# Pooled values of attention split into 112 and 32 tokens, a third column product in an accumulator's bank, and a new issue order

## The chip, the core and the metric

One kernel on one core of a Trainium2 chip. The metric is the device time of one execution in microseconds (us), from the first to the last instruction with the start and end around them. The core has five engines that run their own instruction streams in order: TensorE (PE, matmuls; its weight loads are listed apart as PEld), VectorE (DVE), ScalarE (ACT), GpSimd (POOL) and SyncE (SP, which here only issues transfers). They wait for one another by semaphores.

## The reference

Three layers on 4 x 576 tokens of 512 channels. Attention first, of 32 heads (16 pairs of heads, here called pairs 0 to 15):

```python
q_d = q.reshape(B, H, Sd, factor, D).mean(axis=3)      # factor 4, Sd = 144
k_d, v_d = ...                                          # the same for k and v
out_up = np.repeat(sm_attn(q_d, k_d, v_d), factor, axis=2)
mask = np.abs(pos[:, None] - pos[None, :]) < factor
out_local = softmax(where(mask, scale * q @ k.T, -1e9)) @ v
x = out_up + out_local
```

then a gated layer, `h = relu(x @ w_in)`, `gate = sigmoid(conv3(h))`, `x = (h * gate) @ w_out`, and a mixer, `u = x + (x.T @ U @ V).T`, `out = u + relu(u @ w_ch1) @ w_ch2`. Everything is float32.

## The kernel before

All engines' instructions are written out by hand: `SEQ` is a string of words, and each word calls one small function, so the order of the words is the order of the instructions on each engine. A word is a name with numbers, `V.3.2` is `pv_local(3, 2)`. The words that matter here, p being a pair of heads:

- `lq.p`, `lr.p`, `lw.p` load q and k (576 KB), the values for pooling (`vr`, 288 KB) and the values for the local part (`vw`, 384 KB). `wl.1.i` loads a weight tile (512 KB). All loads go through `load` (L319) on SP's queue, in the order of the words; each waits until those more than 900 units before it have landed, and also for the engine that last read the buffer it overwrites.
- `S.p` scores of the local part (L447 masks, L454 48 small matmuls, each two records in the trace), `dp.p` (L483) and `D.p` (L476) subtract the maxima, `E.p` exponentials, `R.p re.p r.p` row sums, their eps and their reciprocals, `n.p` or `nv.p` the normalisation, `T.p` (L554) three transposes, `c.p` or `cv.p` the copy out of PSUM, `V.p` (L588) 24 matmuls with `vw`.
- `Sd.p` (L520), `Md.p`, `Ed.p` (L532), `nd.p` on POOL or `ndv.p` on DVE (L537) the same for the pooled part with its 144 tokens. `Td.p` (L561) transposes the 96 x 144 weights in six pieces of 72 columns, `cd.p` on ACT or `cdv.p` on DVE (L578) copies them out, `vs.p.i` on POOL or `vsv.p.i` on DVE (L544, L547) sums the four tokens of `vr` in two steps on 72 partitions (tokens 0 to 71 and 72 to 143 beside each other), and `Vd.p` (L596) is four matmuls on 72 partitions. `x.p` (L615) adds both parts into X.
- `1.n.c` (`g1`, L813) is a quarter, three matmuls, of the n-th column product of the gated layer, into one of two PSUM banks, `gx` for even n and `gy` for odd (`gtile`). Its chain on ACT and DVE is `r1.n` (L819), `c0.n` (L835), `c1.n.k` (L840), `th.n` (L844), `gt.n` or `gm.n` (L851), `gh.n` (L856) and `gl.n` on POOL or `gL.n` on DVE (L859). The first eight products use `gt`, which leaves the result in the same PSUM bank until `gL.n` has read it, so product n + 2 can begin only after `gL.n`; `gm` moves it to SBUF. `2.n.c` (`g2`, L867) multiplies the gated block with w_out into accumulators `acc0` to `acc2`, one PSUM bank each.
- `f.n` issues n beats (L389, `beat`), matmuls without a use that are put where PE would stand still; there are 89 in the list. `sp` (L371) is the same ahead of the first loads.

From product `1.0.0` on, attention of the later pairs is interleaved with the column products. After attention and the gated layer come the mixer's stages (L1024, L1056, L1177), whose weights pass through DRAM.

Of the kernel before, what the change touches and what calls it, by code (L numbers as in the profile page):

```python
# [7 lines left out]
F32 = mybir.dt.float32  # L8
# [10 lines left out]
SEQ = ("lq.1 xz sf sp.1 k sp.0 K qs.1 sp.1 S.1.1 lc cw.0 z M.1 lq.0 qs.0 qd.1 Sd.1.0 dp.1 lr.0 E.1 R.1 S.0.2 M.0 vs.0.0 "  # L19
# [253 lines left out]


@with_exitstack
def mixer_kernel(ctx, tc, consts, qk, vw_, vr_, w1, w2, cw_, u_, v_, out, outT):
    nc = tc.nc
    DM = out.shape[1]
    S = qk.shape[3]
# [526 lines left out]
    def g1(n, cc):  # L806
        g, f = divmod(n, NF)
        wd = runs(g)[1]
        if cc == 0:
            gp[n] = gtile(n % 2)  # L810
# [481 lines left out]
```

## Time and profile before

| | |
|---|---|
| time, median of 3 runs | 708.25 us (705.76 to 709.41) |
| the profiled execution's own time | 708.66 us |
| its span, first to last instruction | 706.9 us |
| PE busy | 686.0 us (97%) |
| PE weight loads busy | 630.0 us (89%) |
| DVE busy | 542.2 us (77%) |
| ACT busy | 430.6 us (61%) |
| POOL busy | 348.2 us (49%) |
| mean granted clock of TensorE | 0.992 of 2.4 GHz |
| transfers | 152 MB, 215 GB/s on average |

PE is busy for all but 20.9 us of the span. Times below are us from the span's start. Busy time of an engine is the union of its records; an idle time in a timeline is what lay ahead of the group, with what released it. "issue" means that the engine waited for nothing that the profile shows.

### The profile page before, as it was taken

Reading aid. Unit: us, or ns where it says so; the run is one execution under the profiler, and the core shown is the slowest. Engines: PE = TensorE matmul, PEld = TensorE weight load, DVE = VectorE, ACT = ScalarE, POOL = GpSimd, SP = SyncE. Lnnn points to the kernel's source line nnn. Section 1 sums busy time; section 2 is a strip of 40 time slices with the busy share of each in tenths; the row PEclk is TensorE's granted clock in tenths of the full one; section 3 lists DMA queues with packets and bytes.
Section 4 is the critical chain, followed back from the end, with each engine's and each line's share of the span. In section 5 each row is a group of like instructions: output and inputs, shape, how many; then the busy total and the mean of one; then the engine's idle time right before and its main releaser. Section 6 shows DMA issues by size and latency. Waiting matters only on the chain.

```text
span 706.9 us, 15817 instructions
## 1 busy us (share of the span) xinstructions
PE 686.0 (97%) x5937; PEld 630.0 (89%) x5937; DVE 542.2 (77%) x961; ACT 430.6 (61%) x995; POOL 348.2 (49%) x353
## 2 busy tenths in 40 slices
PE   7868999999999999999999999999999999999997
PEld 5767889888888889898899898899999999999997
DVE  5867999989887776989976856667767798666777
ACT  3777897866696676888655655654343565344431
POOL 2335557542353643467555645253733564544544
PEclk9979999999999999999999999999999999999999
DMA  7877723763553221145778898998687666787865
GB/s 203 275 245 250 266 77 104 242 206 126 169 185 132 74 75 62 60 163 194 254 270 308 285 329 280 298 318 317 230 263 230 249 226 238 231 279 223 283 200 185
DMA packets 74620, 152.09 MB, mean 215 GB/s; under 512 B 8112, under 2 KB 16560, under 8 KB 74544
## 3 DMA queue, kind: packets, MB, share of 16 engines
q1 hardware_dynamic: 74544, 151.09, 64.5%
q8 instruction: 47, 0.77, 0.4%
q14 instruction: 29, 0.24, 0.1%
HBM read 111.21 MB, written 39.85 MB: 214 GB/s over the span
## 4 chain that ended last, share of the span: by engine, by line
PE 81%; DMA 7%; DVE 5%; issue 2%; ACT 2%; POOL 2%; SPq 0%; DVEq 0%; POOLq 0%; ACTq 0%
PE g L1024 22%; PE acc L867 13%; PE g L813 12%; PE xa L1177 9%; PE acc L1056 9%; PE ya L1177 5%; PE za L1177 2%; PE O L588 1%; DMA zraw<-in_w_dram 1%; PE h L891 1%; DMA vr<-in_vr_dram 1%; PE O L596 1%; PE S L454 1%; PE Sd L520 1%; DMA raw<-in_w_dram 1%
## 5 line engine op out<-in xcount | busy, mean ns | idle before, releaser
L1024 PE MATMUL g<-bt,as 128*128 128x384 f32 x1008 | 195.7, 338 | 0.0
L1024 PEld LDWEIGHTS g<-bt,as 128*128 128x128 f32 x1008 | 178.4, 188 | 4.1 <-ACT tp L1029 0.3
L813 PE MATMUL g<-xhl,w 128*128 128x386 f32 (+1 forms) x576 | 116.9, 346 | 1.6 <-DVE ghl L859 1.6
L867 PE MATMUL acc<-w,ghl 128*128 128x512 f32 x432 | 114.2, 397 | 0.0
L813 PEld LDWEIGHTS g<-xhl,w 128*128 128x128 f32 x576 | 102.6, 191 | 7.0 <-DVE ghl L859 1.8
L1163 POOL TENSOR_TENSOR rt<-fr,rt 128x384 fp32r<-128x384 f32 x64 | 66.5, 1050 | 72.8 <-ACT rt L1159 49.5
L1184 DVE TENSOR_TENSOR uT<-uT,xa 128x384 f32<-128x384 f32 x128 | 68.6, 550 | 29.4 <-PE xa L1177 29.1
L867 PEld LDWEIGHTS acc<-w,ghl 128*128 128x128 f32 x432 | 79.3, 188 | 13.0 <-issue 0.4
L1177 PE MATMUL xa<-rt,wb 128*128 128x384 f32 x384 | 82.4, 338 | 2.0 <-DVE uT L1184 1.2
L859 POOL TENSOR_TENSOR ghl<-ct,ghl 128x384 fp32r<-128x384 f32 x40 | 42.9, 1073 | 78.8 <-ACT ghl L856 74.7
L1029 ACT ACTIVATE tp<-g 128x384 f32<-128x384 f32 x72 | 35.1, 488 | 73.4 <-PE g L1024 71.3
L1056 PE MATMUL acc<-w,a 128*128 128x512 f32 x288 | 73.8, 394 | 0.5 <-DVE a L1044 0.5
L1033 DVE TENSOR_TENSOR tp<-g,tp 128x384 f32<-128x384 f32 x72 | 40.0, 555 | 43.2 <-PE g L1024 35.0
L840 DVE SCALAR_TENSOR_TENSOR g<-h,cw,g 128x384 f32<-128x384 f32 x96 | 59.4, 619 | 17.5 <-ACT g L835 16.0
L1163 POOL TENSOR_TENSOR rt<-tp,rt 128x384 fp32r<-128x384 f32 x48 | 50.4, 1057 | 45.0 <-ACT rt L1159 23.1
L1177 PEld LDWEIGHTS xa<-rt,wb 128*128 128x128 f32 x384 | 67.8, 188 | 3.5 <-DVE uT L1184 2.6
L1056 PEld LDWEIGHTS acc<-w,a 128*128 128x128 f32 x288 | 53.2, 188 | 9.6 <-DVE a L1044 0.9
L1159 ACT ACTIVATE rt<-fr 128x384 fp32r<-128x384 f32 x64 | 31.8, 520 | 22.8 <-PE za L1177 8.0
L1177 PE MATMUL ya<-rt,wb 128*128 128x384 f32 x192 | 42.6, 339 | 0.4 <-DVE uT L1184 0.3
L1086 POOL TENSOR_TENSOR l<-s,l 128x256 fp32r<-128x256 f32 x28 | 23.6, 845 | 34.1 <-ACT l L1082 29.8
L1184 DVE TENSOR_TENSOR uT<-uT,ya 128x384 f32<-128x384 f32 x64 | 34.8, 549 | 5.7 <-PE ya L1177 5.5
L819 ACT ACTIVATE h<-g 128x386 f32<-128x386 f32 (+1 forms) x48 | 23.5, 489 | 23.2 <-PE g L813 23.0
(169 smaller groups left out, 1266.4 us busy)
## 6 DMA issues: line engine op xcount, KB each, us to landing
as<-s SPq DMA_DIRECT2D x112, 256.0 KB, 3.3
wb<-t SPq DMA_DIRECT2D x112, 256.0 KB, 4.4
s<-as SPq DMA_DIRECT2D x56, 256.0 KB, 3.0
raw<-in_w_dram SPq DMA_DIRECT2D x26, 512.0 KB, 7.6
zraw<-in_w_dram SPq DMA_DIRECT2D x22, 512.0 KB, 3.5
qk<-in_qk_dram SPq DMA_DIRECT2D x16, 576.0 KB, 6.0
t<-l SPq DMA_DIRECT2D x28, 256.0 KB, 2.7
vw<-in_vw_dram SPq DMA_DIRECT2D x16, 384.0 KB, 3.7
```

Source lines behind the costliest of these rows:

```text
L813: nc.tensor.matmul(gp[n][:, :wd], w[:, a, cc], xhl[g, cc][:, b, :wd], start=cc == 0 and i == 0, stop=cc == NCC - 1 and i == 2)
L840: nc.vector.scalar_tensor_tensor(out=o, in0=inner(g, hts[n], k), scalar=cw[:, k * NF + f:k * NF + f + 1], in1=o, op0=ALU.mult, op1=ALU.add)
L859: eng.tensor_tensor(ghl[n][:, 1], cts.pop(n), ghl[n][:, 0].bitcast(F32), op=ALU.subtract)
L867: nc.tensor.matmul(acc[g][c], t[:, a, c * P:(c + 1) * P], w[:, b], start=f == 0 and i == 0, stop=f == NF - 1 and i == 2)
L1024: nc.tensor.matmul(o, w[:, a, k], Bs[r, j, k][:, b, :TB], start=j in (0, 1, 3) and n == 0, stop=n == 3 * HC - 1, skip_group_check=True)
L1029: nc.scalar.activation(out=t[:, :TB], in_=bank[q, 0][:, :TB], func=AF.Copy)
L1033: nc.vector.tensor_tensor(t, bank[q, 1][:, :TB], t, op=ALU.add)
L1056: nc.tensor.matmul(acc2[g][c], t[:, a, c * P:(c + 1) * P], w[:, b], start=f == 0 and n < 2 and i == 0, stop=f == NFP - 1 and n >= 2 and i ...
L1159: nc.scalar.activation(out=t[:, 0], in_=f_src(q, j), func=AF.Copy)
L1163: eng.tensor_tensor(t[:, 1], f_src(q, j), t[:, 0].bitcast(F32), op=ALU.subtract)
L1177: nc.tensor.matmul(o, w[:, a, m * P:m * P + P], t[:, b], start=new and i == 0, stop=i == 2, skip_group_check=True)
L1184: nc.vector.tensor_tensor(u, u, src, op=ALU.add)
```

## The change

**Pooled values.** Tokens 0 to 111 of a pair now stand on 112 partitions, and the other 32 tokens of four pairs together on 128 partitions (pair p on partitions 32 (p mod 4) onwards). The host writes two inputs: `vr`, 112 partitions x 2 KB a pair (224 KB), and `vz` for pairs 0, 4, 8 and 12, 128 partitions x 4 KB (512 KB), which holds that pair's 112 tokens and the 32 tokens of its four pairs. `vsum` therefore works on half the columns for twelve pairs, and for the four others on 128 partitions. `Td.p` transposes columns 0 to 127 in one piece, and in the other the columns from 112 - 32 (p mod 4) to 143, 32 to 128 of them, so that the last 32 land on the right partitions. `copy_Td` is two copies, 112 x 288 and 32 x 288, but one of 128 x 576 where p mod 4 is 3. `Vd.p` stays four matmuls of 64 x 144, over 112 and 32 partitions.

**Third product.** Product 2 is written to a bank with the tag `acc2`, not `gx`; it uses `gm.2`, which moves its result to SBUF, since `2.0.2` takes this bank.

**Order.** All of `SEQ` is new. It has the same words as before, but for `gm.2` in place of `gt.2`, and the same 89 beats.

```diff
     def load_vr(p):
-        t = st[p]["vr"] = xu.tile([72, 4, 2, 2, D], F32, name="vr", tag=f"xu{4 + p % 2}")
-        load(t.rearrange("p t h c d -> p (t h c d)"), vr_[p], 288)
+        if p % 4:
+            t = st[p]["vr"] = xu.tile([NM, 4, 2 * D], F32, name="vr", tag=f"xu{4 + p % 2}")
+            load(t.rearrange("p t x -> p (t x)"), vr_[p], 2 * NM)
+        else:
+            t = st[p]["vr"] = xu.tile([P, 4, 4 * D], F32, name="vr", tag=f"xu{4 + p % 2}")
+            load(t.rearrange("p t x -> p (t x)"), vz_[p // 4], 512)
...
     def vsum(p, part, eng=None):
...
-            d = e["vd"] = pa.tile([72, 2, 2, D], F32, name="vd", tag="vd", bufs=2)
-            eng.tensor_tensor(d.rearrange("p h c d -> p (h c d)"), t[:, 0], t[:, 1], op=ALU.add)
+            d = pa.tile([P, 4 * D], F32, name="ve", tag="ve", bufs=1)
+            e["vd"] = d[:NM]
+            for i in range(p, p + 4):
+                st[i]["ve"] = d[:, 2 * D:]
+        eng.tensor_tensor(d, t[:, 0], t[:, 1], op=ALU.add)
...
+    def rest(p):
+        return slice(32 * (p % 4), 32 * (p % 4) + 32)
...
     def trans_d(p, n):
-            for c in range(2):
-                nc.tensor.transpose(s[:72, c, 96 * j:96 * j + 96], e["Pd"][:, j, 72 * c:72 * c + 72], ident[:96, :96])
+            nc.tensor.transpose(s[:, 0, to], e["Pd"][:, j, :P], ident[:96, :96])
+            nc.tensor.transpose(s[:rest(p).stop, 1, to], e["Pd"][:, j, NM - rest(p).start:], ident[:96, :96])
...
     def copy_Td(p, copy):
-        copy(t, e.pop("Td")[:72, :, :288])
+        if rest(p).stop == P:
+            copy(t, s[:, :, :288])
+        else:
+            copy(t[:NM, 0], s[:NM, 0, :288])
+            copy(t[rest(p), 1], s[rest(p), 1, :288])
...
     def pv_pooled(p):
-            for c in range(2):
-                nc.tensor.matmul(e["O"][...], e["vd"][:, h, c], pt[:, c, :, 48 * h:48 * h + 48], start=c == 0, stop=c == 1)
+            nc.tensor.matmul(o, e["vd"][:, cols], pt[:NM, 0, :, to], start=True, stop=False)
+            nc.tensor.matmul(o, e["ve"][rest(p), cols], pt[rest(p), 1, :, to], start=False, stop=True)
...
     def g1(n, cc):
-            gp[n] = gtile(n % 2)
+            gp[n] = gtile(n % 2) if n != 2 else pools["psg"].tile([P, 512], F32, name="g", tag="acc2")
```

On PE, after the scores of pairs 1 and 0 (`Sd.0` and `dp.0` are the first two rows). Before:

```order
L520 MATMUL Sd<-ss,qd_100 96x144 x3
L483 MATMUL S<-nm,front 128x192 x2
L389 MATMUL S<-mask,identR 128x224 x15
L447 MATMUL S<-mask,identR 128x192 x2
L454 MATMUL S<-qk 24x32 x48
L554 MATMUL T<-front,P 128x128 x3
```

Now:

```order
L525 MATMUL Sd<-ss,qd_100 96x144 x3
L488 MATMUL S<-nm,front 128x192 x2
L575 MATMUL Td<-front,Pd 128x96
L576 MATMUL Td<-front,Pd 32x96
...
L390 MATMUL S<-mask,identR 128x224
L452 MATMUL S<-mask,identR 128x192 x2
L459 MATMUL S<-qk 24x32 x48
L565 MATMUL T<-front,P 128x128 x3
L390 MATMUL S<-mask,identR 128x224 x14
```

The transposes of pair 0's pooled part (`Td.0`) come ahead of the scores of pair 2, and the 14 beats that stood there come after `T.0`.

On PE, at the largest group of beats, after `V.4` and `Vd.4` (L596; now L617 and L618). Before:

```order
L596 MATMUL O<-PTd,vd 64x144 x4
L520 MATMUL Sd<-ss,qd_100 96x144 x3
L389 MATMUL O<-mask,identR 128x224 x35
L554 MATMUL T<-front,P 128x128 x3
L389 MATMUL O<-mask,identR 128x224 x12
L813 MATMUL g<-xhl,w 128x386 x24
L389 MATMUL S<-mask,identR 128x224
```

Now:

```order
L618 MATMUL O<-PTd,ve 64x144
L834 MATMUL g<-xhl,w 128x386 x3
L565 MATMUL T<-front,P 128x128 x3
L390 MATMUL O<-mask,identR 128x224 x47
L834 MATMUL g<-xhl,w 128x386 x9
L390 MATMUL S<-mask,identR 128x224
```

The 24 matmuls of products 2 and 3 stood behind the beats. Now product 2 is done ahead of them (its last three matmuls are the second row) and product 3 alone follows.

On SP, the first loads, from `lr.0` on. Before:

```order
L319 DMA vr<-in_vr_dram 72x1024
L319 DMA qk<-in_qk_dram 128x1152 x2
L319 DMA vr<-in_vr_dram 72x1024 x2
L319 DMA vw<-in_vw_dram 128x768
L319 DMA qk<-in_qk_dram 128x1152
...
L319 DMA raw<-in_w_dram 128x1024 x2
```

Now:

```order
L320 DMA vr<-in_vz_dram 128x1024
L320 DMA raw<-in_w_dram 128x1024
L320 DMA qk<-in_qk_dram 128x1152
L320 DMA raw<-in_w_dram 128x1024
L320 DMA uvr<-in_u_dram 128x640
L320 DMA vw<-in_vw_dram 128x768
```

Weight tiles (`raw`) and U (`uvr`, 320 KB) now go ahead of the first `vw`. Up to and with the `vw` of pair 3 SP issues before: qk of pairs 0 to 5, vr of pairs 0 to 3, vw of pairs 0 to 3, two weight tiles and the constants (185 KB), 7353 KB in all; now: qk of pairs 0 to 6, vr of pairs 0 to 4, vw of pairs 0 to 3, four weight tiles, U and the constants, 9817 KB.

## Rows read from the trace of the kernel before

**Rows 1.** Busy us and records by stretch; then granted clock, DMA share, GB/s.

```profile
0.00:18.00 18.00, 14.14 (x340) 10.37 (x340) 9.40 (x18) 7.07 (x24) 4.72 (x16) 1.00 0.74 205
18.00:36.00 18.00, 14.66 (x391) 12.38 (x390) 14.57 (x25) 13.97 (x40) 6.33 (x6) 1.00 0.86 269
36.00:54.00 18.00, 13.25 (x236) 11.89 (x237) 11.32 (x21) 12.67 (x37) 6.73 (x7) 0.72 0.72 236
54.00:72.00 18.00, 15.67 (x249) 14.52 (x249) 14.89 (x27) 14.18 (x34) 9.88 (x9) 1.00 0.78 264
72.00:90.00 18.00, 18.00 (x243) 15.91 (x242) 16.77 (x27) 15.90 (x38) 9.55 (x8) 1.00 0.70 254
```

**Rows 2.** PE's timeline, 0 to 72 us: start, us, group, [idle before it].

```profile
14.56 1.93 PE L389 MATMUL S<-mask,identR 128*128 128x224 f32 x15 [1.05 <-ACT P L494]
...
25.60 0.46 PE L596 MATMUL O<-PTd,vd 72*64 72x144 f32 x2 [0.84 <-issue]
...
37.20 0.68 PE L588 MATMUL O<-PT,vw 64*64 64x48 f32 x30 [2.13 <-issue]
...
40.80 0.79 PE L454 MATMUL S<-qk 64*24 64x32 f32 x71
45.05 0.43 PE L454 MATMUL S<-qk 64*24 64x32 f32 x25 [3.46 <-issue]
45.40 1.53 PE L588 MATMUL O<-PT,vw 64*64 64x48 f32 x48
...
50.73 3.00 PE L813 MATMUL g<-xhl,w 128*128 128x386 f32 x9
...
61.63 4.16 PE L389 MATMUL O<-mask,identR 128*128 128x224 f32 x35
...
66.82 1.60 PE L389 MATMUL O<-mask,identR 128*128 128x224 f32 x12 [0.70 <-DVE X L615]
70.04 2.21 PE L813 MATMUL g<-xhl,w 128*128 128x386 f32 x11 [1.62 <-DVE ghl L859]
```

**Rows 3.** The stretches view again, around the fall of the clock.

```profile
42.00:44.00 2.00, 0.00 (x0) 0.00 (x0) 0.00 (x0) 1.39 (x3) 1.74 (x2) 0.80 0.67 208
50.00:52.00 2.00, 2.00 (x9) 2.00 (x9) 1.97 (x6) 1.99 (x10) 0.44 (x1) 0.50 0.38 149
54.00:56.00 2.00, 2.00 (x105) 1.83 (x104) 0.68 (x3) 0.24 (x1) 1.20 (x2) 1.00 0.07 10
```

**Rows 4.** PE's timeline again, between other work.

```profile
55.12 0.49 PE L554 MATMUL T<-front,P 128*128 128x128 f32 x3
55.37 0.77 PE L813 MATMUL g<-xhl,w 128*128 128x386 f32 x3
...
56.55 1.35 PE L813 MATMUL g<-xhl,w 128*128 128x386 f32 x6
57.74 0.66 PE L561 MATMUL Td<-front,Pd 96*72 96x96 f32 x6
58.18 1.31 PE L813 MATMUL g<-xhl,w 128*128 128x386 f32 x6
```

**Rows 5.** Groups of instructions: busy us, mean ns of one, idle before.

```profile
L578 ACT COPY PTd<-Td 72x576 f32<-72x576 f32 x13 | 8.2, 631 | 1.3 <-PE Td L561 1.2
L570 ACT ACTIVATE PT<-T,front 128x288 f32<-128x288 f32 x24 | 10.6, 492 | 1.5 <-PE T L554 1.3
L544 POOL TENSOR_TENSOR vr<-vr 72x512 f32<-72x512 f32 x11 | 15.9, 1446 | 14.3 <-DMA vr<-in_vr_dram 9.7 <-DVE xd L606 4.7
```

**Rows 6.** Timelines of ACT, DVE and POOL: single instructions.

```profile
57.94 0.49 ACT L819 ACTIVATE h<-g 128x386 f32<-128x386 f32 x1 [0.51 <-PE g L813]
...
15.95 0.25 DVE L508 RECIPROCAL sm<-sm 128x15 f32<-128x15 f32 x1 [0.43 <-ACT sm L504]
...
69.44 0.54 DVE L859 TENSOR_TENSOR ghl<-g,ghl 128x384 fp32r<-128x384 f32 x1
...
17.07 0.90 POOL L537 TENSOR_TENSOR Pd<-Pd,sm 96x432 f32<-96x432 f32 x1
```

More of the change, by code (lines that the diff above doesn't have):

```diff
@@ L17 @@
 NEG = -float(2 ** 33)
-SEQ = ("lq.1 xz sf sp.1 k sp.0 K qs.1 sp.1 S.1.1 lc cw.0 z M.1 lq.0 qs.0 qd.1 Sd.1.0 dp.1 lr.0 E.1 R.1 S.0.2 M.0 vs.0.0 "
[249 rows of a table removed]
+SEQ = ("lq.1 xz sf sp.1 k sp.0 K qs.1 sp.1 S.1.1 lc cw.0 z M.1 lq.0 qs.0 qd.1 Sd.1.0 dp.1 lr.0 E.1 S.0.2 qd.0 wl.1.2 "
[250 rows of a table added]
 P = 128
@@ L275, in mixer_kernel @@
 @with_exitstack
-def mixer_kernel(ctx, tc, consts, qk, vw_, vr_, w1, w2, cw_, u_, v_, out, outT):
+def mixer_kernel(ctx, tc, consts, qk, vw_, vr_, vz_, w1, w2, cw_, u_, v_, out, outT):
     nc = tc.nc
@@ L292, in mixer_kernel @@
     WAY, NLIM = 900, 44
-    SD = S // 4
+    SD, NM = S // 4, 112
     SCALE = D ** -0.5
@@ L434, in q_blocks @@
             nc.scalar.activation(out=e["qd"][rows, :, 48 * h:48 * h + 48],
-                                 in_=e.get("sq", e["ss"])[rows, 0].rearrange("p (j r) -> p j r", j=3), func=AF.Copy, scale=SCALE / 16)
+                                 in_=(e["sq"] if "sq" in e else e["ss"])[rows, 0].rearrange("p (j r) -> p j r", j=3), func=AF.Copy, scale=SCALE / 16)
     WS = [min(max(0, NQ * i - 4), S - NW) for i in range(S // NQ)]
@@ L541, in vsum @@
         eng = eng or nc.gpsimd
-        t = e["vr"].rearrange("p t h c d -> p t (h c d)")
+        t = e["vr"]
         if part == 0:
             eng.tensor_tensor(t[:, 0:2], t[:, 0:2], t[:, 2:4], op=ALU.add)
-        else:
-            d = e["vd"] = pa.tile([72, 2, 2, D], F32, name="vd", tag="vd", bufs=2)
-            eng.tensor_tensor(d.rearrange("p h c d -> p (h c d)"), t[:, 0], t[:, 1], op=ALU.add)
+            return
+        if p % 4:
+            d = e["vd"] = pa.tile([NM, 2 * D], F32, name="vd", tag="vd", bufs=2)
+        else:
+            d = pa.tile([P, 4 * D], F32, name="ve", tag="ve", bufs=1)
[3 more added lines that the diff above has]
+        eng.tensor_tensor(d, t[:, 0], t[:, 1], op=ALU.add)
     def trans(p, n):
@@ L559, in trans_d @@
         for j in range(3):
-            for c in range(2):
-                nc.tensor.transpose(s[:72, c, 96 * j:96 * j + 96], e["Pd"][:, j, 72 * c:72 * c + 72], ident[:96, :96])
+            to = slice(96 * j, 96 * j + 96)
+            nc.tensor.transpose(s[:, 0, to], e["Pd"][:, j, :P], ident[:96, :96])
+            nc.tensor.transpose(s[:rest(p).stop, 1, to], e["Pd"][:, j, NM - rest(p).start:], ident[:96, :96])
     def copy_T(p, eng):
@@ L576, in copy_Td @@
         e = st[p]
-        t = e["PTd"] = pa.tile([72, 2, 288], F32, name="PTd", tag="PTd", bufs=1)
-        copy(t, e.pop("Td")[:72, :, :288])
+        t = e["PTd"] = pa.tile([P, 2, 288], F32, name="PTd", tag="PTd", bufs=1)
+        s = e.pop("Td")
+        if rest(p).stop == P:
[3 more added lines that the diff above has]
+            copy(t[rest(p), 1], s[rest(p), 1, :288])
     def pv_local(p, n):
@@ L594, in pv_pooled @@
         for h in range(2):
-            for c in range(2):
-                nc.tensor.matmul(e["O"][D * h:D * h + D, 0, 288:288 + SD].rearrange("p (j r) -> p j r", j=3),
-                                 e["vd"][:, h, c], pt[:, c, :, 48 * h:48 * h + 48], start=c == 0, stop=c == 1)
+            o = e["O"][D * h:D * h + D, 0, 288:288 + SD].rearrange("p (j r) -> p j r", j=3)
+            to, cols = slice(48 * h, 48 * h + 48), slice(D * h, D * h + D)
+            nc.tensor.matmul(o, e["vd"][:, cols], pt[:NM, 0, :, to], start=True, stop=False)
+            nc.tensor.matmul(o, e["ve"][rest(p), cols], pt[rest(p), 1, :, to], start=False, stop=True)
     def copy_od(p, eng):
@@ L1252 @@
     vw = _np.ascontiguousarray(_np.concatenate([vw[..., :2, :], vw[:, ::-1, ..., 2:, :]], axis=5)).reshape(16, 128, 3 * 4 * D)
-    vr = _np.ascontiguousarray(vp.reshape(16, 2, 2, 72, 4, D).transpose(0, 3, 4, 1, 2, 5)).reshape(16, 72, 16 * D)
+    vt = vp.reshape(16, 2, 144, 4, D)
+    vm = vt[:, :, :112].transpose(0, 2, 3, 1, 4)
+    vr = _np.ascontiguousarray(vm).reshape(16, 112, 8 * D)
+    vz = _np.zeros((4, 128, 4, 2, 2, D), vr.dtype)
+    vz[:, :112, :, 0] = vm[::4]
+    vz[:, :, :, 1] = vt[:, :, 112:].transpose(0, 2, 3, 1, 4).reshape(4, 128, 4, 2, D)
+    vz = vz.reshape(4, 128, 16 * D)
     def tiles(a, b):
@@ L1279 @@
     arrays, args = {}, []
-    for name, a in (("consts", consts), ("qk", qk), ("vw", vw), ("vr", vr), ("w1", w1), ("w2", w2), ("cw", cw),
+    for name, a in (("consts", consts), ("qk", qk), ("vw", vw), ("vr", vr), ("vz", vz), ("w1", w1), ("w2", w2), ("cw", cw),
                     ("u", un), ("v", vn)):
```

499 rows, old and new, of the table SEQ are left out of this document.

## The prediction, made before the changed kernel ran

> **What bounds the kernel now.** I read the page's busy times first: PE 686.0 of 706.9 us, so nothing but PE's work, its idle time and its clock can move the end by much. Then the stretches [rows 1]: from 0 to 72 us PE is busy 14.14 + 14.66 + 13.25 + 15.67 = 57.7 us, idle 14.3; from 72 us on it is saturated, and all the rest of the span holds only 20.9 - 14.3 = 6.6 us of idle time. The list has the same matmuls and the same 89 beats as before. So the question is what the new order does to the first 72 us. Third, PE's timeline there [rows 2], for what each idle time waited for. Three gaps name no engine ("issue"): 0.84, 2.13 and 3.46 us. They lie inside runs of small matmuls, and by PE's records they stand at equal distances: from the one ending at 37.20 to the one ending at 45.05 are 128 records, from the one at 25.60 to the one at 37.20 twice that (254, a few records can be missing). A record of PE comes with a weight load, so this is every 256 instructions. I read them as waits for the next block of code: the blocks that end in a gap had been issued in 2.8 to 5 us of work, and the time from one gap's end to the next was 5.1 (for the shorter of the two blocks to 37.20) and 7.85 us, while the DMA engines were busy for 0.86 and 0.72 of the time [rows 1]. Behind the longest gap the granted clock falls to the lower level, 0.50 (1.2 GHz), and is back at 1.00 by 54 us [rows 3]. Nine matmuls of a column product took 3.00 us there [rows 2], against 1.35 for six at full clock [rows 4]: 0.33 each against 0.22. The 8.5 us from 45.05 to 53.6 cost 2.8 us by that ratio of 1.5, 4.3 if all of it ran at half speed; I take 3.7, nearer to the upper end, since these matmuls had other waits for weights at full clock. Last, the wait of 1.62 us for ghl and 0.70 us for X ahead of the third product [rows 2].
>
> On instruction supply the Trainium skill says, in "Runtime: NRT & Kernel Launch", section "Instruction fetch mechanics", that code comes in blocks of 256 instructions, the next one fetched while the current one runs, and that crossing a block is mostly hidden. The block size fits the distances here; that it is hidden does not, with 3.46 us in one crossing.
>
> **The change part by part.** *Third product.* Before, `1.2.0` needs the bank that `gL.0` frees, and PE fills the time with 35 + 12 beats and still waits 0.70 + 1.62 us. Now the 12 matmuls of product 2 run ahead of the beats in a bank of their own: -2.3. What is late next? `1.3.0`, which needs `gL.1`. In the trace product 0's chain took from its relu at 57.94 to the end of its ghl at 69.98, 12.0 us [rows 6]; product 1's is taken as no longer. Now PE has, between the end of product 1 and `1.3.0`, 47 beats (at 4.0 us for 35, 61.63 to 65.63, 5.4 us), seven quarters of products 0 and 2 (0.6 each by 56.55 to 57.74 for two [rows 4], 4.2), and the scores and values of two pairs (155 records at 0.011 us by 0.79 for 71, 1.7), with Td and two T (1.0): 12.3 us, and the four groups `dp.5`, `dp.6`, `Sd.6`, `Vd.4` besides. No wait there. `2.0.0` needs `gL.0`: from the end of product 0 PE has 5.4 us of beats, eight quarters (4.8), one pair's values and one pair's scores (1.7) and Td and T (1.0), 12.9 against 12.0, but on DVE nine instructions stand between `gL.1` and `gL.0`, decodes among them. I take +0.5, with ends 0 and 2. Product 2's accumulator `2.0.2` comes right behind, after `gm.2`, which stands ahead of `gL.0` on DVE: nothing more.
>
> *Loads.* Up to the `vw` of pair 3 there are now 9817 KB, 10.05 MB, not 7353 KB. At the measured rates 205 x 18 + 269 x 18 = 8.53 MB have moved by 36 us, the rest takes 6.4 us at 236 GB/s, and with some 1 us to land `V.3` can start at about 43.5. Before, `V.3` started at 45.40, just after the 3.46 us gap: -1.9 net of that gap. I take the code gap itself as covered there: the block of 128 records that ends in the scores of pair 5 now also holds `V.3`, `Vd.3`, six matmuls of products and the wait for the load. If PE doesn't stand still for as long as 3.46 us, the clock doesn't fall: -3.7.
>
> *Other gaps.* `Td.0` now comes right behind `dp.0` and waits for `nd.0` on POOL. By the trace the reciprocal ended at 16.2 and POOL takes 0.90 [rows 6], so `Td.0` starts near 17, where before the 14 beats covered the time from 14.56 to pair 2's scores. PE stands some 3 us there. It costs nothing by itself as long as `V.3` waits for its load, and is the first place where the clock could fall. One block (`Td.2`, `Sd.4`, `S.4` and part of `V.2`) is still as short as the one that ended in the 2.13 gap, and the block from pair 5's to pair 6's scores is some 5 us: a new wait for code of between 0 and 2.8 us (7.85 - 5.1); I take +1.5.
>
> *Transposes.* Six Td with 72 columns of weights and 96 of data took 0.44 us (57.74 to 58.18), three T with 128 and 128 took 0.25 (55.12 to 55.37) [rows 4]: 0.073 and 0.083 each. A Td with 128 weight columns lies between, and for its partner with 32 to 128 columns I take 0.073 and 0.083 at most. By those two rows alone the price is 0 to 6 x 0.01 x 16 = 1.0 us; by columns (168 in 0.073) the first piece gives 0.024 more and the second on average 0.003, 3 x 0.027 x 16 = 1.3. I take +1.1. The four matmuls of `Vd` keep columns and number: 0.
>
> The Trainium skill, in "TensorE: Matmul & The Clock Gate", section "Step-by-step: what each phase is for", has the weight load's time grow with columns and not with rows, and lets it be pulled ahead under a running matmul. Pulled ahead fully the wider pieces would cost nothing, and the sum would be 1.1 lower.
>
> *Copies and sums.* `copy_Td` becomes two copies for twelve pairs: at 0.49 each by the copy of 128 x 288, 0.98 against 0.63 [rows 5], +0.35 on ACT or DVE, 4 us over 200 us in which PE is the later engine: 0 (it is 0 to 2 if DVE, 16.77 of 18 us busy from 72 on [rows 1], has no cover left). `vsum` gets about half as long for twelve pairs (1.45 now on POOL [rows 5]); POOL is busy 49%: 0.
>
> *Sum.* -2.3 + 0.5 - 1.9 - 3.7 + 1.5 + 1.1 = -4.8 from the profiled execution's 708.66 (a span of 706.9 and 1.8 around it): 703.9. The median is 0.4 lower, so 703.5.
>
> **The rivals.** *All gaps go* (699.0): the more even mix of small and large matmuls hides every block of code, so 0.84 and 2.13 go as well and the new 1.5 doesn't come, 4.5 less. Against it: one block is as short as before.
>
> *The clock falls elsewhere* (707.2): PE's pause ahead of `Td.0`, or one for `vw` of pair 2 or 3, brings the same half speed, +3.7. For it: both pauses have no beats in front, and 3.46 us were enough once; against it: a pause of 2.13 us left the clock at 1.00.
>
> *The third product brings nothing* (705.8): the beats are still there, and `1.3.0` waits for its bank as `1.2.0` did, since ACT has more decodes and weight copies ahead of `gh.1` than it had ahead of `gh.0`; +2.3.
>
> *Gaps are not code* (707.0): if crossing a block were hidden, the gaps would have another cause that stays, and only the third product, the gate, the transposes and about half of the clock's share remain, -2.3 + 0.5 + 1.1 - 0.5 = -1.2. This is the Trainium skill's rule cited above.
>
> *Loads too late* (713.8, slower): the 2464 KB put ahead of pair 3's `vw` push it past 47 us, which needs the mean rate up to there to be 214 GB/s, between the 205 of the first stretch and the 236 of the third [rows 1]. PE then stands for `V.2` and for `V.3`, and the clock falls in two stretches. From 708.25: +1.6 for `V.3` at 47.0, +3.7 for the second stretch, +1.5, +1.1, -2.3: 713.8. It decides from the point where `V.3` starts after about 46 us with a pause of over 3 us.
>
> **How the numbers follow.** Forecast 0.38, all gaps go 0.12, the clock elsewhere 0.17, third product 0.10, gaps not code 0.05, loads 0.18. A measurement of this kernel can tell about 0.5% from no change, 704.7 to 711.8. Faster is the forecast and the first rival, 0.50; within are the next three, 0.32; slower the loads, 0.18. The forecast's own range is 700 to 706.5 with the ends of the code gap, the gate and the clock's share. The wide one reaches from 698.5 to 712.5 and leaves out about half of the slow case and a little of the first rival.
>
> **What would show it.** Right: no idle of over 2.5 us on PE between 18 and 60 us, granted clock 1.00 in 36 to 54, `V.3` starting before 44, `1.3.0` without a wait for ghl, PE's idle time up to `2.0.0` near 9 us. Wrong: "issue" gaps of over 3 us at other records, a stretch at 0.50, a wait for ghl ahead of `1.3.0` or `2.0.0`, or idle time on PE beyond 90 us, where DVE with its two copies would be late.

## The result, and the profile after

The changed kernel took 717.35 us (median of 4 runs, 712.53 to 718.54) beside 707.64 us for the kernel before (4 runs, 705.76 to 709.41): ratio 1.012, 95% interval 1.008 to 1.016. It is slower by about 1.2%; the forecast was 703.5 us, with a range that ended at 712.5.

The first lines of the page after (busy time, share of the span, instructions):

```profile
span 716.1 us, 15851 instructions
...
PE 701.1 (98%) x5937; PEld 636.6 (89%) x5937; DVE 543.5 (76%) x963; ACT 433.2 (60%) x1005; POOL 340.7 (48%) x353
```

PE is idle for 716.1 - 701.1 = 15.0 us, 5.9 less than before, but busy for 15.1 us more with the same number of instructions. So this time the loss doesn't stand in a gap; it is inside groups that count as busy. The stretches view after, with the columns of [rows 1]:

```profile
0.00:18.00 18.00, 12.33 (x231) 8.32 (x231) 7.98 (x16) 7.58 (x24) 3.89 (x14) 1.00 0.84 291
18.00:36.00 18.00, 18.00 (x454) 15.62 (x454) 15.67 (x28) 13.46 (x38) 5.19 (x6) 0.91 0.70 221
36.00:54.00 18.00, 16.68 (x302) 13.18 (x289) 14.16 (x21) 13.03 (x37) 7.78 (x8) 0.72 0.74 253
54.00:72.00 18.00, 17.15 (x255) 15.57 (x254) 14.66 (x26) 15.65 (x41) 10.79 (x11) 1.00 0.74 257
72.00:90.00 18.00, 16.74 (x226) 13.76 (x225) 17.58 (x27) 14.49 (x32) 8.55 (x9) 1.00 0.54 174
```

PE's idle time up to 72 us has shrunk from 14.3 to 7.8 us, and yet the span is 716.1 - 706.9 = 9.2 us longer. One pair's `Vd` on PE's timeline after (start, us, group), where the next pair's `Sd` follows:

```profile
24.25 0.46 PE L617 MATMUL O<-PTd,ve 112*64 112x144 f32 x2
24.64 0.45 PE L618 MATMUL O<-PTd,ve 32*64 32x144 f32 x2
25.02 0.46 PE L617 MATMUL O<-PTd,ve 112*64 112x144 f32 x2
25.41 0.45 PE L618 MATMUL O<-PTd,ve 32*64 32x144 f32 x2
25.79 0.49 PE L525 MATMUL Sd<-ss,qd 128*96 128x144 f32 x2
```

and the weight loads of the same matmuls (PEld's timeline, with the idle time before each):

```profile
24.25 0.19 PEld L617 LDWEIGHTS O<-PTd,ve 112*64 112x64 f32 x2
24.64 0.19 PEld L618 LDWEIGHTS O<-PTd,ve 32*64 32x64 f32 x2 [0.20 <-issue]
25.02 0.19 PEld L617 LDWEIGHTS O<-PTd,ve 112*64 112x64 f32 x2 [0.20 <-issue]
25.41 0.19 PEld L618 LDWEIGHTS O<-PTd,ve 32*64 32x64 f32 x2 [0.20 <-issue]
```

Before, the eight records of a `Vd` were one run of weight loads without a pause (PEld's timeline of the kernel before):

```profile
83.31 0.45 PEld L596 LDWEIGHTS O<-PTd,vd 72*64 72x64 f32 x8
83.95 0.30 PEld L813 LDWEIGHTS g<-xhl,w 128*128 128x128 f32 x2 [0.20 <-issue]
```

Groups overlap at their ends, so I read a length from a group's start to the next one's start. Before, `Vd` is 83.95 - 83.31 = 0.64 us. After, it is 25.79 - 24.25 = 1.54 us: each of the four matmuls takes 0.385 us, and each weight load behind a change of rows waits 0.20 us. The other pairs have the same two lengths to within 0.02 us, but for a few with a wait or half clock in them or behind them. That is 0.90 x 16 = 14.4 us for work that the prediction had put at 0. The theory to test: PE finishes what is in it when the number of rows of neighbouring matmuls changes from 112 to 32 or back, and doesn't load the next weights under the running matmul; before, all four had 72 rows.

### The profile page after: what moved, and what is told of

Same layout as the page of the kernel before. It is cut to its first block, busy times and chain, and to the rows that moved or that the text cites. A ratio compares the mean times of both kernels' runs of the same rounds, so it can differ in the third digit from the quotient of the medians.

```text
span 716.1 us, 15851 instructions
## 1 busy us (share of the span) xinstructions
PE 701.1 (98%) x5937; PEld 636.6 (89%) x5937; DVE 543.5 (76%) x963; ACT 433.2 (60%) x1005; POOL 340.7 (48%) x353
## 4 chain that ended last, share of the span: by engine, by line
PE 89%; DMA 3%; DVE 2%; issue 2%; POOL 2%; ACT 1%; SPq 1%; DVEq 0%; POOLq 0%; ACTq 0%
PE g L1045 24%; PE acc L888 14%; PE g L834 13%; PE acc L1077 9%; PE xa L1198 8%; PE ya L1198 4%; PE za L1198 2%; PE O L608 2%; PE O L617 1%; PE S L459 1%; PE Sd L525 1%; PE O L618 1%; DMA wb<-t 1%; PE h L912 1%; POOL w L721 1%
## 5 line engine op out<-in xcount | busy, mean ns | idle before, releaser
L834 PE MATMUL g<-xhl,w 128*128 128x386 f32 (+1 forms) x576 | 119.0, 346 | 0.8 <-DVE ghl L880 0.8
L721 POOL TENSOR_TENSOR w<-wval,w 128x512 fp32r<-128x512 f32 x17 | 22.8, 1348 | 28.7 <-ACT w L718 22.8
```

The source lines that it names most:

```text
L834: nc.tensor.matmul(gp[n][:, :wd], w[:, a, cc], xhl[g, cc][:, b, :wd], start=cc == 0 and i == 0, stop=cc == NCC - 1 and i == 2)
```

## The experiments

Each ratio is against runs of the kernel before on the same chip at the same time. Their medians were 705.75, 706.41 and 706.49 us on the three chips.

**Vd grouped by row count** (the changed kernel):

```diff
-        for h in range(2):
-            matmul(o(h), vd[:, cols(h)], pt[:112, 0, :, to(h)], start=True, stop=False)
-            matmul(o(h), ve[rest(p), cols(h)], pt[rest(p), 1, :, to(h)], start=False, stop=True)
+        for c in range(2):
+            for h in range(2):      # c = 0: the 112-row matmul of half h, c = 1: the 32-row one
+                ...
```

> The changed kernel, with the four matmuls of each pair's Vd issued as both 112-row ones, then both 32-row ones, so the same work in another order. Theory (a change of row count between neighbouring matmuls stops PE: three more changes per pair than before cost 0.89 us, 0.30 each): two of the three go, 2 x 0.30 x 16 = 9.5 us, 717.4 becomes about 708, and Vd takes about 0.95 us per pair instead of 1.54. Rival (a 32-row matmul is slow by itself, 0.44 us each): nothing changes, 717.

Measured: 707.26 us, ratio 1.002 (0.999 to 1.005). `Vd` on PE's timeline:

```profile
24.62 0.47 PE L619 MATMUL O<-PTd,ve 112*64 112x144 f32 x4
25.02 0.46 PE L621 MATMUL O<-PTd,ve 32*64 32x144 f32 x4
25.41 0.98 PE L525 MATMUL Sd<-ss,qd 128*96 128x144 f32 x6
```

Here it is 0.79 us, and the same four matmuls in another order bring back 717.35 - 707.26 = 10.1 us between the medians, 8.2 us when each is compared with the kernel before beside it (9.7 and 1.5 us above it). The theory holds, though not its flat price of 0.30 per change: the first change costs 0.79 - 0.64 = 0.15 us, the two further ones 0.75 together. A group of two records and one of four take about the same 0.39 us.

How that can be is seen in how many records run at once. Here is the stretches view of `Vd`'s matmuls alone, about 0.05 to 0.15 us after a `Vd` has begun (PE busy us and records; then clock, DMA share, GB/s), in the kernel before, in the grouped version and in the changed kernel:

```profile
83.35:83.45 0.10, 0.10 (x2) 1.00 1.20 481
80.35:80.45 0.10, 0.10 (x2) 1.00 0.00 0
84.05:84.15 0.10, 0.10 (x1) 1.00 0.00 0
```

Two matmuls run side by side before and in the grouped version; in the changed kernel each runs alone. So four records of one row count are two matmuls at once, which take no longer than one. The 0.90 us hold both this loss and the waits of the weight loads; no run separates the two.

**32 rows throughout** (the kernel before):

```diff
-    e["vd"][:, h, c], pt[:, c, :, 48 * h:48 * h + 48]
+    e["vd"][:32, h, c], pt[:32, c, :, 48 * h:48 * h + 48]
```

> The kernel before, with all four matmuls of Vd on the first 32 of their 72 rows; the other 40 rows' share of the product is left out. Theory (changes of the row count): no change of rows inside Vd, so its 0.65 us per pair and 707.6 us stay. Rival (32-row matmuls are slow by themselves): four slow ones per pair where the changed kernel has two, 4 x 0.44 x 16 = 28 us, 736 us.

Measured: 705.89 us, ratio 1.001 (0.999 to 1.004). `Vd` and what follows it:

```profile
87.98 0.71 PE L596 MATMUL O<-PTd,vd 32*64 32x144 f32 x8
88.63 0.59 PE L389 MATMUL O<-mask,identR 128*128 128x224 f32 x3
```

0.65 us with 32 rows as with 72. A matmul over 32 rows is not slow; the rival falls.

**72 and 32 rows in turn** and **72 and 68 rows in turn** (the kernel before, second matmul of each half):

```diff
-    e["vd"][:, h, c], pt[:, c, :, 48 * h:48 * h + 48]
+    e["vd"][:(72, 32)[c], h, c], pt[:(72, 32)[c], c, :, 48 * h:48 * h + 48]    # or (72, 68)
```

> The kernel before, with the second matmul of each half of Vd on 32 of its 72 rows (the other 40 rows' share is left out), so that 72 and 32 rows alternate. Theory (the change of rows between the large and the 32-row form stops PE): Vd 1.54 us per pair, 706 + 14 = 720. Rival (the cost belongs to something else in the split by 112 and 32, such as the shared tile ve, its place on partitions 0 to 127, or the two copies): 706.

> The kernel before, with the second matmul of each half of Vd on 68 of its 72 rows (the last four rows' share is left out): the row count changes between neighbours three times per pair, as in the changed kernel, but only from 72 to 68. Theory in its narrow form (any change of the row count stops PE): Vd about 1.54 us per pair, 16 x 0.89 = 14 us more, 720. Rival (only a change between a count above and one at or below 32 stops it, as between 112 and 32): 0.65 us per pair and the time of before, 706.

Measured: 719.35 us, ratio 1.018 (1.011 to 1.025), with 32; 706.56 us, ratio 1.000 (0.996 to 1.003), with 68. First the version with 32, then that with 68:

```profile
80.96 1.62 PE L596 MATMUL O<-PTd,vd 72*64 72x144 f32 x8
82.51 3.96 PE L813 MATMUL g<-xhl,w 128*128 128x386 f32 x21
```

```profile
81.86 0.72 PE L596 MATMUL O<-PTd,vd 72*64 72x144 f32 x8
82.50 3.96 PE L813 MATMUL g<-xhl,w 128*128 128x386 f32 x21
```

1.55 us against 0.64. The price needs neither the shared tile nor the two copies nor the new list; and the theory's narrow form is wrong: not any other number of rows, but a change between two classes of it. 112, 72 and 68 on the one side and 32 on the other lie in different classes; 72 and 68 lie in one. Counts between 33 and 64 were not run.

The version with 68 rows also shows which matmuls run side by side. Its lines view from 81.85 to 82.10 us has four records of 72 rows and none of 68:

```profile
L596 PE MATMUL O<-PTd,vd 72*64 72x144 f32 x4 | 0.5, 312 | 0.0
```

In the program two records of 72 rows and two of 68 for half 0 stand ahead of those for half 1. So the 72-row matmul of half 1 ran beside that of half 0, ahead of half 0's 68-row one.

**Rows crossed with halves** (the changed kernel), so that neighbours don't add onto the same half of the output at two of the three changes:

```diff
-    112 rows half 0, 32 rows half 0, 112 rows half 1, 32 rows half 1
+    112 rows half 0, 32 rows half 1, 112 rows half 1, 32 rows half 0
```

> The changed kernel, with Vd's matmuls as 112 rows of half 0, 32 rows of half 1, 112 rows of half 1, 32 rows of half 0: still three changes of the row count inside Vd, but at two of them the neighbours write different halves of the output. Theory (each change of the row count stops PE, whatever the output): Vd stays near 1.54 us per pair. Rival (the stop comes from adding onto the half that the matmul just ahead is still writing): only the middle change costs 0.3, Vd falls to about 1.0 us per pair and the time by about 8 us, to 709.

Measured: 716.80 us, ratio 1.014 (1.009 to 1.019).

```profile
27.53 0.46 PE L618 MATMUL O<-PTd,vd 112*64 112x144 f32 x2
...
29.08 0.73 PE L525 MATMUL Sd<-ss,qd 128*96 128x144 f32 x4
```

1.55 us again, so it isn't the accumulation. Neighbours of different halves don't run side by side here either (one record from 82.15 to 82.25 us), since their rows differ.

**Halves in turn** (the kernel before, all 72 rows):

```diff
         for h in range(2):
             for c in range(2):
# becomes
         for c in range(2):
             for h in range(2):
```

> The kernel before, with the loops of Vd exchanged, so that neighbouring matmuls write different halves of the output (both 72-row ones of the first 72 tokens, then both of the second). Theory (only changes of the row count matter): 0.65 us per pair and the time of before, ratio 1.000. Rival (matmuls on different halves overlap, since a group of four records took 0.40 in the grouped version and one of two records 0.39 in the changed kernel): Vd falls to 0.50 or less, 16 x 0.15 = 2.4 us, ratio 0.997.

Measured: 706.33 us, ratio 1.000 (0.997 to 1.003), and 0.64 us per `Vd`:

```profile
88.11 0.71 PE L596 MATMUL O<-PTd,vd 72*64 72x144 f32 x8
88.75 0.59 PE L389 MATMUL O<-mask,identR 128*128 128x224 f32 x3
```

This doesn't speak against an overlap of the two halves: they run two records at a time in this order (from 79.65 to 79.75 us) as in the order before, so the exchange had nothing to win.

**Pooled values alone**, in turn and grouped (the list and the third product's bank of the kernel before):

```diff
-SEQ = (the changed kernel's list)
+SEQ = (the list before)
-            gp[n] = gtile(n % 2) if n != 2 else pools["psg"].tile([P, 512], F32, name="g", tag="acc2")
+            gp[n] = gtile(n % 2)
```

> The kernel before with its own list and its own tile for the third product, and only the pooled values split by 112 and 32. Theory: Vd costs 14.2 us more and Td 1.1 us more, 707.6 + 15.3 = 723. Rival (the loss of the changed kernel comes from its list): about 709.

> The kernel before with its own list, and only the pooled values split by 112 and 32, with Vd's matmuls grouped by row count. Theory: Vd 0.79 us per pair as in the grouped version against 0.65, 16 x 0.14 = 2.2 us, and Td 1.1 us: 706 + 3.3 = 709. The list is then worth the difference to the grouped version's 707.3, about 2 us, and not the 5.9 us by which PE's idle time was lower in the changed kernel. Rival (the list is worth what the changed kernel's idle time shows): this version comes at 713.

Measured: 721.60 us, ratio 1.024 (1.022 to 1.026), in turn; 710.74 us, ratio 1.005 (1.000 to 1.009), grouped. The split of the pooled values is the whole loss and more; grouping wins 10.9 us of it (11.6 when each is compared with the kernel before beside it), by the working 16 x 0.75 = 12.0.

**The list and the third product alone** (pooled values 72 and 72):

```diff
-SEQ = (the list before)
+SEQ = (the changed kernel's list, with vs.11.1 moved behind Vd.8 and vsv.14.1 behind Vd.12)
-            gp[n] = gtile(n % 2)
+            gp[n] = gtile(n % 2) if n != 2 else pools["psg"].tile([P, 512], F32, name="g", tag="acc2")
```

> The changed kernel's list and its third column product's tile, with the pooled values split 72 and 72 as before (the second step of the sums of pairs 11 and 14 moved behind Vd.8 and Vd.12, since there are two buffers). Theory (the list brings what the idle time of PE shows, 20.9 to 15.0 us, and the loss lies in Vd and Td): 707.6 - 5.9 = about 702. Rival (the list itself loses, for instance by its loads): 707.6 or more.

Measured: 710.27 us, ratio 1.006 (1.004 to 1.009). A miss: 8 us above what the idle time had promised. The granted clock of its runs was lower too, 0.988 in the median against 0.995 for the kernel before beside it, so a part of the miss can lie there. Its page and two of its waits:

```profile
PE 689.8 (97%) x5937; PEld 633.2 (89%) x5937; DVE 544.6 (77%) x961; ACT 430.5 (61%) x995; POOL 345.7 (49%) x353
```

```profile
73.73 0.49 PE L618 MATMUL acc<-w,ghl 128*128 128x512 f32 x1 [1.56 <-DVE ghl L610]
...
186.36 0.92 PE L339 MATMUL O<-PT,vw 64*64 64x48 f32 x48 [1.71 <-DMA vw<-in_vw_dram]
```

PE is idle for 708.8 - 689.8 = 19.0 us there, and for 706.3 - 686.0 = 20.3 us in the grouped version, against 20.9 before. So with a short `Vd`, with or without the new split, the list saves 0.6 to 1.9 us of idle time, not 5.9. The wait of 1.56 us is 0.45 in the changed kernel. Nor does a slow `Vd` alone shorten the idle time as much: with the list before it leaves 719.7 - 700.5 = 19.2 us (pooled values alone, in turn) and 716.5 - 696.5 = 20.0 (72 and 32 rows in turn). Only both together have 15.0, and 714.4 - 700.9 = 13.5 in the version with rows crossed. That other engines catch up in the new list while PE takes longer would fit this; no run shows it.

**The third product alone** (the kernel before):

```diff
+ 1.2.0 1.2.1 1.2.2 1.2.3 r1.2 c0.2        (ahead of f.10 f.6 f.19)
+ c1.2.1 c1.2.2 th.2 gm.2                  (behind gL.1; both runs taken from their later places, gt.2 is gm.2)
-            gp[n] = gtile(n % 2)
+            gp[n] = gtile(n % 2) if n != 2 else pools["psg"].tile([P, 512], F32, name="g", tag="acc2")
```

> The kernel before, with its list and pooled values, where only the third column product is moved: its 12 matmuls and its relu stand ahead of the 35 beats, in the bank of the third accumulator, and its gate is moved to its own buffer (gm.2) behind gL.1. By the prediction's term the waits of 0.70 and 1.62 us go, ratio 0.997 (2.3 of 706 us). Rival (the idle time turns up again at the next place where PE waits, as the idle time of 19 to 20 us in the grouped and the list-only versions suggests, against 20.9 before): ratio 1.000.

Measured: 710.82 us, ratio 1.008 (1.005 to 1.011), worse than either theory. PE's timeline at `1.3.0`, and the stretch after it:

```profile
68.67 4.22 PE L564 MATMUL g<-xhl,w 128*128 128x386 f32 x12 [3.24 <-DVE ghl L610]
```

```profile
70.00:72.00 2.00, 2.00 (x8) 2.00 (x7) 1.66 (x3) 2.00 (x5) 0.00 (x0) 0.50 0.21 82
```

The wait of 1.62 us for `gL.0` became one of 3.24 us for `gL.1`, followed by half clock: twelve matmuls took 72.70 - 68.67 = 4.03 us. In this list, moving the product ahead only moves the wait.

**Beats ahead of Td.0** (the changed kernel, `Vd` grouped):

```diff
- ... nv.1 lq.2 nd.0 Td.0.2 ...
+ ... nv.1 lq.2 nd.0 f.26 Td.0.2 ...
```

> The changed kernel with Vd grouped, and 26 beats (3.0 us at full clock) put ahead of Td.0, where PE waited 3.26 us for Pd. Theory (the fall of the clock to 0.50 at 14 to 22 us follows PE's idle time there): the stretch from 17 to 22 us shows 1.00, and the time falls by 1 to 2 us against 707.3. Rival (the fall has its cause elsewhere): the stretch keeps 0.50 to 0.70 and the time is the same or longer.

Measured: 710.97 us, ratio 1.005 (1.003 to 1.008). One stretch of the grouped version and then of this one, and two groups of this one's timeline:

```profile
18.00:20.00 2.00, 2.00 (x72) 1.81 (x73) 2.00 (x3) 1.58 (x4) 1.36 (x2) 0.50 0.72 258
```

```profile
18.00:20.00 2.00, 2.00 (x107) 1.94 (x79) 1.97 (x5) 2.00 (x5) 0.00 (x0) 1.00 0.95 275
```

```profile
30.58 0.77 PE L275 MATMUL Sd<-ss,qd 128*96 128x144 f32 x5 [2.02 <-issue]
...
39.41 0.90 PE L315 MATMUL T<-front,P 128*128 128x128 f32 x3 [1.84 <-POOL P L268]
```

With the pause of 3.26 us filled, the clock stays at 1.00 where it had been 0.50, so that fall goes with PE's idle time there. In the grouped version that was not the pause alone: an "issue" gap of 2.36 us ended just ahead of it, at 13.70, and is 0.23 us here. The changed kernel had the fall with 0.96 us there. The time gets no better: PE is ahead by 1.5 us at pair 2's `Sd` (23.88 against 25.41) and behind the grouped version again (34.94 against 34.76) at the scores of pair 4, after an "issue" gap of 2.02 us. Behind the wait of 1.84 us the clock falls in this version (0.50 from 40 to 42 us); in the grouped one it stayed at 1.00 behind 1.39 us at the same place.

## Why the prediction failed, point by point

**The step that failed** is the sentence "The four matmuls of `Vd` keep columns and number: 0". Columns and number were the wrong things to count. The rows of the neighbours decide whether the next weights are loaded under the running matmul and whether the two halves run side by side: +0.90 x 16 = 14.4 us by the trace, 8 to 10 us won back by another order of the same instructions, and 12.9 us lost by 72 and 32 rows in turn in the old kernel. With this term the forecast would have been 703.5 + 14.4 = 717.9 beside the measured 717.35. That it comes so close is partly luck: the terms for the clock and for Td failed too, and what the list brings depends on `Vd`, as below. No rival held this mechanism, so the range had no room for it either. The 112 and 32 rows side by side were there to be read in the change as described ahead of the prediction; the trace of before held a hint too, the 0.20 us for which PEld waits where `Vd` ends and matmuls of another shape begin (83.95 above). What changes there is the weight columns, from 64 to 128, with 72 and 128 rows. Behind transposes of 72 columns PEld loads the same 128 without a wait (kernel before):

```profile
58.16 0.48 PEld L813 LDWEIGHTS g<-xhl,w 128*128 128x128 f32 x3
```

So columns may have classes as well; no run changed them alone. The Trainium skill states the rule, in "TensorEngine Tiling (Array Packing)", sections "Key Properties" and "Available Configurations": a change of the tiling mode drains TensorE, and modes go by 128, 64 or 32 rows. The runs agree as far as they go: 72 and 68 rows act as one mode and 32 as another, with 0.15 us for one change inside a `Vd` and 0.90 for three; 112 rows beside 72 were not run.

**Clock, -3.7: failed.** The pause of 3.46 us is gone, but the stretch from 36 to 54 us is at 0.72 on average, the same as in [rows 1]. PE's timeline after:

```profile
17.35 0.30 PE L575 MATMUL Td<-front,Pd 96*128 96x96 f32 x1 [3.26 <-POOL Pd L542]
...
39.91 0.55 PE L565 MATMUL T<-front,P 128*128 128x128 f32 x3 [1.08 <-POOL P L518]
...
43.05 1.53 PE L608 MATMUL O<-PT,vw 64*64 64x48 f32 x48
...
71.33 1.76 PE L834 MATMUL g<-xhl,w 128*128 128x386 f32 x9
...
75.97 0.50 PE L888 MATMUL acc<-w,ghl 128*128 128x512 f32 x1 [0.45 <-DVE ghl L880]
```

`Td.0` waited 3.26 us (about 3 was forecast), and behind it the clock fell, with 0.50 from 18 to 20 us and 0.69 from 20 to 22: the rival "the clock falls elsewhere", which the 26 beats bear out with the reserve stated there. From 41.7 to 52 us it fell again, after waits of only 1.08 and 0.24 us, for which I have no cause.

**Gaps, +1.5 net of the code that is covered: near in size, wrong in place.** The gaps of 0.84, 2.13 and 3.46 us at their old records are gone; the one new gap, of 0.96 us at 13.44, lies in neither of the two blocks that the prediction named. And their length is no property of the list. The same instruction as in [rows 2] at 37.20, in the versions with 32 rows throughout and with 72 and 32 in turn:

```profile
36.62 0.67 PE L588 MATMUL O<-PT,vw 64*64 64x48 f32 x30 [2.99 <-issue]
```

```profile
36.11 0.67 PE L588 MATMUL O<-PT,vw 64*64 64x48 f32 x30 [1.07 <-issue]
```

It stands before the same matmul each time, with 2.13, 2.99 and 1.07 us; the gap of 3.46 is absent in the first of these versions and 1.38 in the second. The lengths that the forecast used came from one execution. What does hold is the distance that the prediction read. These are PE's records from the start up to such a gap (the columns as above), for 37.20 in the kernel before, 30.58 in the version with beats ahead of `Td.0` and 13.44 in the changed kernel:

```profile
0.00:37.15 37.15, 28.81 (x729) 1.00 0.80 238
0.00:30.50 30.50, 25.03 (x602) 1.00 0.86 284
0.00:13.40 13.40, 11.03 (x221) 1.00 0.81 282
```

In all thirteen traces every such gap of 0.25 us or more stands behind 221, 475, 602, 729, 857 or 984 records, 127 or 128 apart or twice that, whichever matmul comes next there. That they are waits for code fits this and is not shown.

**Third product, -2.3: right in the new list, wrong by itself.** `1.3.0` starts at 71.33 without a wait for ghl; a wait of 0.85 us for X stays ahead of the beats (0.70 before). Alone, the move costs 0.8%.

**`gL.0`, +0.5: right.** 0.45 us at 75.97. **`V.3`, -1.9: right in its place** (43.05; 43.5 was forecast, 45.40 before), but what it won doesn't show in the end of the span in the runs of the list without the slow `Vd`.

**Td, +1.1: wrong, it is 0.** In the grouped pooled version six pieces of 128 and 64 columns take 74.81 - 74.37 = 0.44 us ahead of a product, as 57.74 to 58.18 in [rows 4]:

```profile
74.37 0.25 PE L574 MATMUL Td<-front,Pd 96*128 96x96 f32 x1
...
74.81 1.64 PE L890 MATMUL acc<-w,ghl 128*128 128x512 f32 x6
```

The rule of the Trainium skill that the prediction set against its own price (weight loads pulled ahead under the matmul, "TensorE: Matmul & The Clock Gate", section "Step-by-step: what each phase is for") gave 0, and the trace agrees. The expectations of the pooled versions, which still held 1.1 us for Td, were that much too high in their working.

**Copies and sums, 0: held.** PE's waits after hold none for the copies of `Td` (0.2 us in the grouped version); POOL's busy time fell by 7.5 us and brought nothing.

**The list as a whole** is the least settled part. It is worth about 1.2% where `Vd` is slow (1.012 against 1.024), something between nothing and little where `Vd` is grouped (1.002 against 1.005, intervals overlap), and the list costs 0.6% with the old split and two sums moved. Which of its moves loses what was not separated. No version beat the kernel before.

## What to carry to other kernels

Before splitting a contraction, write down the rows of each matmul beside those of its neighbours: three changes between a large count and 32 cost 0.90 us here, more than the four matmuls between them (0.64), so matmuls of one row class should stand together. Compare PE's busy time for the same instructions as well as its idle time: a loss inside "busy" shows first in the weight loads' waits. And don't book idle time that vanishes while PE gets slower as a gain of one part of a change: here 5.9 us went with the list and the slow `Vd` together, and at most 1.9 with either alone.

## What the runs showed of the hardware that I had not expected

- Two matmuls on different halves of the output run side by side when their rows are of one class: both take 0.40 us together, and four such matmuls 0.64. One between neighbours of another row class runs alone and takes 0.385 us at full clock.
- The ten longest pauses of PE in the traces (2.45 to 3.46 us, in nine of them) all had half clock in them or right behind; of the shorter ones some had, others not: 1.08 us in the changed kernel had, 1.39 us at the same place in the grouped version hadn't. The kernel before alone ranged from 703.83 to 712.81 us on one chip, and its longer runs had the lower mean granted clock (0.986 in the longest, 0.996 in the shortest), so a median needs more than a few executions.
- The gaps without a named cause stand at fixed counts of PE's records but last differently from one version and execution to the next: 1.07, 2.13 and 2.99 us before the same matmul.
